# Experts 2 to 7: row tiles by way of DRAM and VectorE instead of TensorE's transposes

## The chip, the cores and the metric

The kernel runs on one core of a Trainium2 chip. The time is the device time of one execution in microseconds; a comparison goes by the median of several runs of each kernel on the same chip. Engines are named as in the profile: PE is TensorE (PEld its weight loads), DVE VectorE, ACT ScalarE, POOL GpSimd, and SP SyncE, which issues nearly all DMAs. Where the row of an engine ends in q (SPq, PEq), it is that engine's queue.

## What is computed

Three stages follow each other: linear attention, a mixture of eight experts with two experts per token, and a feed-forward block whose two weight matrices are given in 64-bit floats.

```python
def _moe_ref(x, w_gate, w_noise, noise, w1, w2):
    logits = x @ w_gate
    noisy_logits = logits + np.log1p(np.exp(x @ w_noise)) * noise
    top2 = np.argpartition(-noisy_logits, 2, axis=1)[:, :2]
    ...
    for e in range(E):
        for k in range(2):
            mask = top2[:, k] == e
            h = np.maximum(x[mask] @ w1[e], 0.0)
            out[mask] += top2_w[mask, k, None] * (h @ w2[e])

def _moe2_ref(x, w_in, w_out, g_ln):
    h = x @ w_in
    solu = h * softmax(h)
    ...
    return (layernorm(solu) * g_ln) @ w_out

def reference(...):
    x = attention(q, k, v)           # 2304 tokens, 512 features
    x = _moe_ref(x, ...)             # 8 experts, 512 -> 1024 -> 512
    return _moe2_ref(x, ...)         # 512 -> 1024 -> 512
```

## The kernel before

**Products.** A number is split into a high part (32 bits, rounded for TensorE, written by ScalarE) and a low part (the rest, by a VectorE subtraction), and a product is three matmuls: high by high, high by low, low by high.

**Experts.** Attention's result lies in DRAM (`xd`). Each expert has 640 slots in five tiles of 128 tokens. `gather_x` lets GpSimd fetch the 128 rows of a tile by an indirect DMA into a buffer `xg` (tokens on partitions, 512 features along the row). `xt_tile` calls `transpose_split`: four TensorE transposes of 128 by 128 by way of a PSUM bank `t`, then ScalarE writes the high part `xh` and VectorE the low part `xl`, features on partitions. `mm1(e, m)`, m = 0 to 7, is the first product: eight blocks of 128 of the 1024 hidden features, each two halves of 320 tokens with 12 matmuls. Behind each block ScalarE takes the relu (`hh`), and VectorE the rest (`hl`); only the latter frees the block's PSUM bank `a`, of which there are two. `mm2(e, a)`, a = 0 to 4, is the second product: 24 matmuls for one tile of tokens, whose result `yo` is copied by VectorE (even a) or ScalarE (odd a) and stored to DRAM (`yd`).

**Order.** The schedule is written out by hand: engines run their instructions in the order of the code. Attention, routing and expert 0 stand in a table (`ORDER`); then a loop runs experts 1 to 7. In step m of the first product stand `mm1(e, m)`, for m below 4 the split of a quarter of w2 and `load_w1(e + 1, m)`, for m below 5 `gather_x(e + 1, m)`, and from m = 3 on one piece of the decode (`next(bg)`). In step a of the second product stand `xt_tile(e + 1, a)`, `mm2(e, a)`, a piece of the decode, and for a below 4 the split of a quarter of w1 for the next expert and the load of a quarter of its w2.

**Decode.** `decode_all` turns the 64-bit w_in and w_out into 32-bit floats while the experts run: 16 tiles, each loaded by SyncE into one of two buffers `f`, worked on by nine VectorE instructions in four pieces (tiles `dec`) and stored to DRAM. The first piece issues the loads of the first two tiles, the second begins to work on the first of them. It is in expert 1, at m = 3 and 4.

**Buffers.** A ring hands out named buffers in turn, and an instruction that writes one waits until its last reader is through. `raw` (weights as loaded) is a ring of four, `xg` one of five, and `dec` takes three of a ring of four.

**Tail.** Behind the experts, the 18 token tiles of the feed-forward block already turn most of their tiles in another way: the tile is written to DRAM (`d_write`), read back in four pieces of 32 partitions (`d_read`), and turned by VectorE in blocks of 32 by 32 (`d_back`). The weights in that stage are loaded in the row order that goes with it.

Of the kernel before, what the change touches and what calls it, by code (L numbers as in the profile page):

```python
# [8 lines left out]
F32 = mybir.dt.float32  # L9
# [3 lines left out]
U32 = mybir.dt.uint32  # L13
# [7 lines left out]
NT, DM, FF, E = 2304, 512, 1024, 8  # L21
# [3 lines left out]
KD, KF = DM // 128, FF // 128  # L25
NA = 5
# [27 lines left out]

NP = 2

ORDER = """
F:100011101100000000100000000000101111 lk:0 lq:0 lkl:0 lk:1 kr:0 kmt:0 qm:0 lvl:0 km:0:0 klt:0 kl:0 km:0:1 kb:0
lk:2 kr:1 qs:0 lv:0 rz:0 ks:0 kmt:1 ksl:0 qe:0 kr:2 km:1:0 T:0 kmt:2 rz:1 km:1:1 C:0 kb:1 lkl:1 rz:2 T:1 km:2:0
# [25 lines left out]
def attn_moe_kernel(ctx: ExitStack, tc: tile.TileContext, q, k, v, w_gate, w_noise, noise,  # L85
                    w1, w2, w_in, w_out, g_ln, out, order=None, stop=False):
    nc = tc.nc
    V, A, P, T, SP = nc.vector, nc.scalar, nc.gpsimd, nc.tensor, nc.sync
# [5 lines left out]
    dram = ctx.enter_context(tc.tile_pool(name="dram", bufs=1, space=DRAM))  # L94
    sb = ctx.enter_context(tc.tile_pool(name="sb", bufs=1))

    def slot(tag, shape, dt, name):
        return sb.tile(shape, dt, tag=tag, name=name)

    def ring(*tags):  # L100
        state = [-1]

        def take(shape, dt, name):
            state[0] = (state[0] + 1) % len(tags)
            return slot(tags[state[0]], shape, dt, name)
        return take

    new_raw = ring("R2", "R3", "R0", "R1")
    new_row = ring("S0", "S2", "S4", "S1", "S3")
    new_out = ring("S9", "S8", "S10")  # L110
    new_s2 = ring("S5", "S6", "S7", "S11")
    psA = ctx.enter_context(tc.tile_pool(name="psA", bufs=2, space=PSUM))
    psB = ctx.enter_context(tc.tile_pool(name="psB", bufs=2, space=PSUM))
# [4 lines left out]
    tab = dram.tile([OVT * 128, 2], I32, name="tab")  # L118
    win32 = dram.tile([DM, FF], F32, name="win32")
    wout32 = dram.tile([FF, DM], F32, name="wout32")  # L120
    dd = {t: dram.tile([128, FF], F32, name=f"dd{t}") for t in range(NP, NC - 2)}

    def bank_t():
        return psT.tile([128, 512], F32, tag="t", name="t")
# [19 lines left out]

    def load_w1(e, j):
        t = new_raw([128, KD, 256], F32, "raw")
        src = win32 if e == E else w1[e]
        SP.dma_start(out=t, in_=src[:, 256 * j:256 * j + 256].rearrange("(k p) f -> p k f", p=128))
        raw[1, e, j] = t

    def load_w2(e, j):
        t = new_raw([128, 2, 512], F32, "raw")
        if e < E:
            SP.dma_start(out=t, in_=w2[e][256 * j:256 * j + 256, :].rearrange("(k p) d -> p k d", p=128))
        else:
            for g in range(4):
                r = 256 * g + 64 * j
                SP.dma_start(out=t[32 * g:32 * g + 32], in_=wout32[r:r + 64, :].rearrange("(k c) d -> c k d", c=32))
        raw[2, e, j] = t
# [26 lines left out]
    def dec_src(i):  # L186
        if i < 8:
            r, c = divmod(i, 2)
            return w_in, win32, slice(128 * r, 128 * r + 128), 512 * c
        return w_out, wout32, slice(128 * (i - 8), 128 * (i - 8) + 128), 0  # L190
# [7 lines left out]
    def decode(i):  # L198
        _, dst, rs, c0 = dec_src(i)
        t = d64.pop(i).rearrange("p (c w) -> p c w", w=2)  # L200
        lw, hw = t[:, :, 0], t[:, :, 1]
        a, b, c = (new_s2([128, 512], U32, f"dec{j}") for j in range(3))
        V.tensor_scalar(b, hw, 3, 0x3FFFFFF8, op0=OP.logical_shift_left, op1=OP.bitwise_and)
        V.scalar_tensor_tensor(a, hw, 0xC0000000, b, op0=OP.bitwise_and, op1=OP.bitwise_or)
        V.scalar_tensor_tensor(a, lw, 29, a, op0=OP.logical_shift_right, op1=OP.bitwise_or)
        yield

        V.tensor_scalar(b, lw, 0x1FFFFFFF, 6, op0=OP.bitwise_and, op1=OP.logical_shift_right)
        V.tensor_scalar(c, a, 0xFF800000, None, op0=OP.bitwise_and)
        V.tensor_tensor(b, b, c, op=OP.bitwise_or)  # L210
        yield
        af, bf, cf = (x.bitcast(F32) for x in (a, b, c))
        V.tensor_sub(bf, bf, cf)
        V.scalar_tensor_tensor(af, bf, 2.0 ** -23, af, op0=OP.mult, op1=OP.add)
        yield

        V.tensor_scalar(c, hw, 20, 0x7FF, op0=OP.logical_shift_right, op1=OP.bitwise_and)
        V.scalar_tensor_tensor(af, c, 896.5, af, op0=OP.is_ge, op1=OP.mult)
        SP.dma_start(out=dst[rs, c0:c0 + 512], in_=af)
# [245 lines left out]
    eTs, xs = {}, {}  # L465
# [68 lines left out]
    Gt = {}  # L534
# [170 lines left out]
    def count_overflow():  # L705
        ps = bank_t()[:, 0:E]
        count(ps, [M16[:, i] for i in range(NC)] + [skip], True, True)
        V.tensor_copy(CT, ps)
        o = const.tile([128, E], F32, name="ovc")
        m = const.tile([128, E], I32, name="ovm")  # L710
        s = const.tile([128, 1], F32, name="ovs")
        V.tensor_scalar(o, CT, -float(CAP), 0.0, op0=OP.add, op1=OP.max)
        V.tensor_scalar(o, o, 127.0, None, op0=OP.add)
        V.tensor_copy(m, o)
        V.tensor_scalar(m, m, 127, None, op0=OP.bitwise_and)
        V.tensor_sub(o, o, m)
        V.reduce_sum(s, o, axis=AX)
        V.tensor_scalar(novi, s, 1.0 / 128.0, None, op0=OP.mult)


    xg = {}

    def gather_x(e, a):
        t = new_row([128, DM], F32, "xg")
        c = E * a + e
        first = e == 0 and a < TA
        P.indirect_dma_start(out=t, out_offset=None, in_=xd[0:NRA, :] if first else xd, in_offset=bass.IndirectOffsetOnAxis(  # L727
            ap=idxA[:, a:a + 1] if first else idx[:, c:c + 1], axis=0))
        xg[e, a] = t

    def transpose_split(t, hi, lo):
        ps = bank_t()
        for kk in range(KD):
            T.transpose(ps[:, 128 * kk:128 * kk + 128], t[:, 128 * kk:128 * kk + 128], ident)  # L734
        pv = ps.rearrange("p (k t) -> p k t", k=KD)
        A.copy(hi, pv)  # L736
        V.tensor_sub(lo, pv, hi)  # L737

    XT = {}

    def xt_tile(e, a):
        if a == 0:
            XT[e] = (slot("XH", [128, KD, CAP], F32R, "xh"), slot("XL", [128, KD, CAP], F32R, "xl"))
        hi, lo = XT[e]
        transpose_split(xg.pop((e, a)), hi[:, :, 128 * a:128 * a + 128], lo[:, :, 128 * a:128 * a + 128])

    hT = {}

    def mm1(e, m):
        hi, lo = XT[e]  # L750
        pa = bank_a()
        j, o = m // 2, 128 * (m % 2)
        for n in range(2):
            for kk in range(KD):
                wh, wl = W1h[j][:, kk, o:o + 128], W1l[j][:, kk, o:o + 128]
                xh, xl = hi[:, kk, HC * n:HC * n + HC], lo[:, kk, HC * n:HC * n + HC]
                for s, (a, b) in enumerate(((wh, xh), (wh, xl), (wl, xh))):
                    T.matmul(pa[:, n, 0:HC], lhsT=a, rhs=b, start=(kk == 0 and s == 0),  # L758
                             stop=(kk == KD - 1 and s == 2))
        h, l = h_tiles(m)  # L760
        h2, l2 = (x.rearrange("p (n c) -> p n c", n=2) for x in (h, l))
        A.activation(out=h2, in_=pa[:, :, 0:HC], func=AF.Relu)  # L762
        V.scalar_tensor_tensor(l2, pa[:, :, 0:HC], 0.0, h2, op0=OP.max, op1=OP.subtract)  # L763
# [340 lines left out]
    def stepwise(f):  # L1104

        def step(*a):
            if a[-1] == 0:
# [13 lines left out]
                  lv2=lambda j: load_w2(1, j), hx=lambda a: gather_x(1, a), xu=lambda a: xt_tile(1, a))  # L1121
    for op in (order or ORDER).split():
        f, *a = op.split(":")
# [5 lines left out]
    for e in range(1, E):  # L1129
        for m in range(KF):  # L1130
            mm1(e, m)
            if m < 4:
                split_w2(e, m)
                load_w1(e + 1, m)
            if e + 1 < E and m < NA:
                gather_x(e + 1, m)
            if m >= 3:
                next(bg, None)
            if e == 2 and m == 5:
                pair_gates()  # L1140
                count_overflow()
        if stop:
            return
        for a in range(NA):
            if e + 1 < E:
                xt_tile(e + 1, a)
            mm2(e, a)
            if e < E - 1:
                next(bg, None)
                if a < 4:  # L1150
                    split_w1(e + 1, a)
                    load_w2(e + 1, a)
                continue
            gather_y(a)
            if a < 2:
                for j in (2 * a, 2 * a + 1):
                    split_w1(E, j)
                    load_w2(E, j)
            elif a == 2:
                next(bg, None)  # L1160
                combine(0)
                split_w2(E, 0)
            elif a == 3:
                x2_trans(0)
                combine(1)
                split_w2(E, 1)
# [69 lines left out]
```

## Time and profile before

| | us |
|---|---|
| median of 3 runs | 807.34 |
| lowest and highest | 806.57 and 809.58 |
| the profiled execution | 807.68 |
| its span, first to last instruction | 806.0 |
| TensorE busy in it | 758.2 |
| VectorE, ScalarE, GpSimd busy | 501.2, 293.8, 144.6 |

The span is what the trace covers; the profiled execution's own time has what lies around it too. The mean granted clock of TensorE is 0.982 of full speed. Matmuls overlap each other, so a matmul's duration is not what it costs in the stream; that is the distance between starts.

### The profile page before, as it was taken

Reading aid. Unit: us, or ns where it says so; the run is one execution under the profiler, and the core shown is the slowest. Engines: PE = TensorE matmul, PEld = TensorE weight load, DVE = VectorE, ACT = ScalarE, POOL = GpSimd, SP = SyncE. Lnnn points to the kernel's source line nnn. Section 1 sums busy time; section 2 is a strip of 40 time slices with the busy share of each in tenths; the row PEclk is TensorE's granted clock in tenths of the full one; section 3 lists DMA queues with packets and bytes.
Section 4 is the critical chain, followed back from the end, with each engine's and each line's share of the span. In section 5 each row is a group of like instructions: output and inputs, shape, how many; then the busy total and the mean of one; then the engine's idle time right before and its main releaser. Section 6 shows DMA issues by size and latency. Waiting matters only on the chain. (4 is left out here: it accounts for less than half of the span.)

```text
span 806.0 us, 12480 instructions
## 1 busy us (share of the span) xinstructions
PE 758.2 (94%) x4934; PEld 684.0 (85%) x4934; DVE 501.2 (62%) x884; ACT 293.8 (36%) x486; POOL 144.6 (18%) x130
## 2 busy tenths in 40 slices
PE   2877869999999999999999999999999999999997
PEld 1777867989789889889899899899898899989985
DVE  6998773334656656556556646546457767767661
ACT  1656531323223323223223232232345354444451
POOL 3684564020110110110200100000342111100000
PEclk9998888999999999999999999999999999999999
DMA  9973444265363454454543552432844545553311
GB/s 274 278 236 119 145 157 139 75 205 157 119 195 107 139 173 144 157 166 136 169 132 121 182 180 94 157 108 76 231 124 146 169 145 158 157 157 131 114 44 39
DMA packets 81534, 119.98 MB, mean 149 GB/s; under 512 B 14912, under 2 KB 52800, under 8 KB 81472
## 3 DMA queue, kind: packets, MB, share of 16 engines
q1 hardware_dynamic: 75392, 99.22, 38.6%
q0 software_dynamic: 6080, 19.93, 9.1%
q8 instruction: 39, 0.64, 0.3%
q14 instruction: 23, 0.19, 0.1%
HBM read 87.67 MB, written 31.46 MB: 148 GB/s over the span
## 5 line engine op out<-in xcount | busy, mean ns | idle before, releaser
L758 PE MATMUL a<-xh,w1h 128*128 128x320 f32 x448 | 138.5, 309 | 1.2 <-DVE hl L763 1.2
L758 PE MATMUL a<-xl,w1h 128*128 128x320 f32 x448 | 138.4, 309 | 0.0
L758 PE MATMUL a<-xh,w1l 128*128 128x320 f32 x448 | 138.3, 309 | 0.0
L794 PE MATMUL b<-w2h,hh 128*128 128x512 f32 x320 | 128.7, 402 | 0.0
L794 PE MATMUL b<-w2h,hl 128*128 128x512 f32 x320 | 126.7, 396 | 0.0
L794 PE MATMUL b<-w2l,hh 128*128 128x512 f32 x320 | 126.3, 395 | 0.0
L762 ACT ACTIVATE hh<-a 128x640 fp32r<-128x640 f32 x56 | 39.6, 707 | 159.8 <-PE a L758 159.8
L727 POOL DMA_INDIRECT xg<-xd,idx x38 | 40.7, 1071 | 304.1 <-PE t L734 294.3
L763 DVE SCALAR_TENSOR_TENSOR hl<-a,hh 128x640 fp32r<-128x640 f32 x56 | 46.1, 824 | 65.0 <-ACT hh L762 64.9
L758 PEld LDWEIGHTS a<-xh,w1h 128*128 128x128 f32 x448 | 84.2, 188 | 1.8 <-DVE hl L763 1.4
L758 PEld LDWEIGHTS a<-xl,w1h 128*128 128x128 f32 x448 | 84.1, 188 | 0.4
L758 PEld LDWEIGHTS a<-xh,w1l 128*128 128x128 f32 x448 | 84.2, 188 | 0.0
L817 POOL DMA_INDIRECT yg<-yd,posi x36 | 35.0, 973 | 208.6 <-DVE w1l L164 100.1
L794 PEld LDWEIGHTS b<-w2h,hl 128*128 128x128 f32 x320 | 60.0, 187 | 13.9
L794 PEld LDWEIGHTS b<-w2l,hh 128*128 128x128 f32 x320 | 60.2, 188 | 13.0
L794 PEld LDWEIGHTS b<-w2h,hh 128*128 128x128 f32 x320 | 60.2, 188 | 12.6
L164 DVE TENSOR_TENSOR w1l<-raw,w1h 128x1024 fp32r<-128x1024 f32 x32 | 38.9, 1222 | 33.4 <-ACT w1h L163 33.4
L842 PE MATMUL a<-w1h,x2h 128*128 128x256 f32 x288 | 57.5, 281 | 1.2 <-ACT x2h L736 0.7
L842 PE MATMUL a<-w1h,x2l 128*128 128x256 f32 x288 | 57.0, 279 | 0.0
L842 PE MATMUL a<-w1l,x2h 128*128 128x256 f32 x288 | 56.8, 278 | 0.0
L796 DVE COPY yo<-b 128x512 f32<-128x512 f32 x24 | 16.6, 692 | 64.2 <-PE b L794 64.2
L925 PE MATMUL b<-w2x,dT 128*128 128x512 f32 x216 | 54.3, 400 | 0.0
(209 smaller groups left out, 1399.3 us busy)
## 6 DMA issues: line engine op xcount, KB each, us to landing
raw<-in_moe_w_dram SPq DMA_DIRECT2D x64, 512.0 KB, 3.7
yd<-yo SPq DMA_DIRECT2D x40, 256.0 KB, 2.0
dd<-ed SPq DMA_DIRECT2D x14, 512.0 KB, 2.6
dq<-dd SPq DMA_DIRECT2D x56, 128.0 KB, 3.8
k<-in_k_dram SPq DMA_DIRECT2D x4, 1024.0 KB, 8.0
q<-in_q_dram SPq DMA_DIRECT2D x4, 1024.0 KB, 8.0
v<-in_v_dram SPq DMA_DIRECT2D x4, 1024.0 KB, 10.6
xd<-xr SPq DMA_DIRECT2D x8, 512.0 KB, 2.6
```

The lines of the kernel that those rows point to most:

```text
L164: (pick_engine(20 + j, P, V) if e == 0 else V).tensor_sub(W1l[j], t, W1h[j])
L727: P.indirect_dma_start(out=t, out_offset=None, in_=xd[0:NRA, :] if first else xd, in_offset=bass.IndirectOffsetOnAxis(ap=idxA[:, a:a + 1] ...
L758: T.matmul(pa[:, n, 0:HC], lhsT=a, rhs=b, start=(kk == 0 and s == 0), stop=(kk == KD - 1 and s == 2))
L762: A.activation(out=h2, in_=pa[:, :, 0:HC], func=AF.Relu)
L763: V.scalar_tensor_tensor(l2, pa[:, :, 0:HC], 0.0, h2, op0=OP.max, op1=OP.subtract)
L794: T.matmul(pb, lhsT=x, rhs=y, start=(kk == 0 and s == 0), stop=(kk == KF - 1 and s == 2))
L796: (A.copy if a % 2 else V.tensor_copy)(t, pb)
L817: P.indirect_dma_start(out=r, out_offset=None, in_=yd[0:n, :], in_offset=bass.IndirectOffsetOnAxis(ap=posi[:, c, j:j + 1], axis=0))
L842: T.matmul(pa[:, n, 256 * c:256 * c + 256], lhsT=x[:, kk, :], rhs=w[2 * n + c][:, kk, :], start=(kk == 0 and s == 0 and c == 0), stop=(kk ...
L925: T.matmul(pb, lhsT=x[:, kk, :], rhs=w, start=(kk == 0 and s == 0), stop=(kk == KF - 1 and s == 2))
```

## The change

For experts 2 to 7 (`EQ = 2`) a tile of rows takes another way to `xh` and `xl`. It is gathered into one of three other buffers (`new_hop`), written to a DRAM tile of its own (`write_x`), and read back in four pieces (`read_x`): the piece g of 32 partitions gets features 128 g to 128 g + 127 of all 128 tokens, in runs of 128 floats. VectorE turns the tile in blocks of 32 by 32 into `xt`, so that features stand on partitions, and the split reads `xt` in SBUF where it read PSUM. On partition 32 g + c, place k, stands feature 128 g + 32 k + c; `load_w1` for these experts therefore loads w1 in the same order, by four DMAs of 32 partitions where there was one of 128. The write of tile m - 1 and the reads of tile m - 3 stand in step m of the first product, behind the load of w1 and ahead of the decode. `decode` takes its result tile from S5 and S6 in turn, and its scratch tiles are always S7 and S11.

```diff
+EQ = 2
...
+    new_hop = ring("RH0", "RH1", "RH2")
...
+    xs_d = {(e, a): dram.tile([128, DM], F32, name=f"xs{e}_{a}") for e in range(EQ, E) for a in range(NA)}
...
-        src = win32 if e == E else w1[e]
-        SP.dma_start(out=t, in_=src[:, 256 * j:256 * j + 256].rearrange("(k p) f -> p k f", p=128))
+        src = (win32 if e == E else w1[e])[:, 256 * j:256 * j + 256]
+        if e < EQ or e == E:
+            SP.dma_start(out=t, in_=src.rearrange("(k p) f -> p k f", p=128))
+        else:
+            for g in range(4):
+                SP.dma_start(out=t[32 * g:32 * g + 32], in_=src[128 * g:128 * g + 128].rearrange("(k c) f -> c k f", c=32))
...
-        a, b, c = (new_s2([128, 512], U32, f"dec{j}") for j in range(3))
+        a, b, c = (slot(tag, [128, 512], U32, f"dec{j}") for j, tag in enumerate((("S5", "S6")[i % 2], "S7", "S11")))
...
-        t = new_row([128, DM], F32, "xg")
+        t = (new_row if e < EQ else new_hop)([128, DM], F32, "xg")
...
+    def write_x(e, a):
+        SP.dma_start(out=xs_d[e, a], in_=xg[e, a])
+
+    def read_x(e, a):
+
+        t = xg[e, a] = new_row([128, DM], F32, "xg")
+        for g in range(4):
+            SP.dma_start(out=t[32 * g:32 * g + 32].rearrange("i (b f) -> i b f", b=4),
+                         in_=xs_d[e, a].rearrange("(b i) f -> i b f", i=32)[:, :, 128 * g:128 * g + 128])
...
-        transpose_split(xg.pop((e, a)), hi[:, :, 128 * a:128 * a + 128], lo[:, :, 128 * a:128 * a + 128])
+        hi, lo = (x[:, :, 128 * a:128 * a + 128] for x in XT[e])
+        t = xg.pop((e, a))
+        if e < EQ:
+            transpose_split(t, hi, lo)
+            return
+        x = slot(("S12", "Gt")[a % 2], [128, KD, 4, 32], F32, "xt")
+        V.transpose(x.rearrange("p k b i -> p b k i"), t.rearrange("p (b k c) -> p b k c", b=4, k=KD))
+        x = x.rearrange("p k b i -> p k (b i)")
+        A.copy(hi, x)
+        V.tensor_sub(lo, x, hi)
...
+            if EQ <= e + 1 < E:
+                if 1 <= m < NA + 1:
+                    write_x(e + 1, m - 1)
+                if 3 <= m:
+                    read_x(e + 1, m - 3)
```

Two places show what it moves. On SyncE's queue, in expert 1 from the last load of w1 for expert 2 (m = 3) to the first loads of the decode; names in brackets are the counters that an issue waits for, DMAHW0 to DMAHW7 those of SyncE's transfers in turn, DMASW those of GpSimd's. Before:

```order
L148 DMA raw<-in_moe_w_dram 128x4x256 [waits DMAHW1_49,DVE_49]
L148 DMA raw<-in_moe_w_dram 128x4x256 [waits DMAHW2_49,DVE_49]
L195 DMA f_1930<-in_moe_w_in_dram 128x1024 [waits DMAHW3_49]
L195 DMA f_1932<-in_moe_w_in_dram 128x1024 [waits DMAHW4_49]
L219 DMA win_78<-dec_1963 128x512 [waits DMAHW5_49,DVE_49]
```

In the changed kernel:

```order
L156 DMA raw<-in_moe_w_dram 32x4x256 [waits DMAHW5_49,DVE_49]
L156 DMA raw<-in_moe_w_dram 32x4x256 [waits DMAHW6_49]
L156 DMA raw<-in_moe_w_dram 32x4x256 [waits DMAHW7_49]
L156 DMA raw<-in_moe_w_dram 32x4x256 [waits DMAHW0_49]
L740 DMA xs_2_82<-xg 128x512 [waits DMAHW1_49,DMASW4_49]
L746 DMA xg<-xs_0_80 32x4x128 [waits DMASW5_49,DMAHW2_49,DMASW0_49,PE_49]
L746 DMA xg<-xs_0_80 32x4x128 [waits DMAHW3_49]
L746 DMA xg<-xs_0_80 32x4x128 [waits DMAHW4_49]
L746 DMA xg<-xs_0_80 32x4x128 [waits DMAHW5_49]
L203 DMA f_1980<-in_moe_w_in_dram 128x1024 [waits DMAHW6_49]
L203 DMA f_1982<-in_moe_w_in_dram 128x1024 [waits DMAHW7_49]
```

One issue of w1 has become four, and a write and four reads have come between it and the loads `f`; each issue waits for the counter that the eighth issue before it used.

On VectorE, in the second product of expert 2, from the split of the first quarter of w1 to the subtraction of the third tile. Before:

```order
L213 TENSOR_TENSOR dec_2543<-dec_2543,dec_2544 128x512
L214 SCALAR_TENSOR_TENSOR dec_2542<-dec_2543,dec_2542 128x512
L164 TENSOR_TENSOR w1l_98<-raw,w1h_94 128x1024
L737 TENSOR_TENSOR xl<-t,xh 128x4x128
L217 TENSOR_SCALAR dec_2544<-f_2228 128x512
L218 SCALAR_TENSOR_TENSOR dec_2542<-dec_2544,dec_2542 128x512
L164 TENSOR_TENSOR w1l_99<-raw,w1h_95 128x1024
L737 TENSOR_TENSOR xl<-t,xh 128x4x128
```

In the changed kernel:

```order
L221 TENSOR_TENSOR dec_2637<-dec_2637,dec_2638 128x512
L222 SCALAR_TENSOR_TENSOR dec_2636<-dec_2637,dec_2636 128x512
L172 TENSOR_TENSOR w1l_128<-raw,w1h_124 128x1024
L768 STREAM_TRANSPOSE xt<-xg 128x4x4x32
L771 TENSOR_TENSOR xl<-xt,xh 128x4x128
L225 TENSOR_SCALAR dec_2638<-f_2288 128x512
L226 SCALAR_TENSOR_TENSOR dec_2636<-dec_2638,dec_2636 128x512
L172 TENSOR_TENSOR w1l_129<-raw,w1h_125 128x1024
L768 STREAM_TRANSPOSE xt<-xg 128x4x4x32
L771 TENSOR_TENSOR xl<-xt,xh 128x4x128
```

Ahead of each subtraction `xl` stands the transpose of the same tile, with nothing between the two.

## Rows read from the trace of the kernel before

**Rows 1.** The page, part 1: busy time of each engine, share, instructions.
```profile
PE 758.2 (94%) x4934; PEld 684.0 (85%) x4934; DVE 501.2 (62%) x884; ACT 293.8 (36%) x486; POOL 144.6 (18%) x130
```

**Rows 2.** Waits of TensorE, 200 to 560 us: us in total, times, longest.
```profile
PE a L758 <- DVE hl L763: 1.2, 1, 1.2
```

**Rows 3.** Timeline of TensorE: start, duration, engine, line, operation, names, shapes, count.
```profile
400.06 0.40 PE L794 MATMUL b<-w2h,hl 128*128 128x512 f32 x1
400.29 0.60 PE L734 MATMUL t<-ident,xg 128*128 128x128 f32 x4
...
400.96 0.39 PE L794 MATMUL b<-w2l,hh 128*128 128x512 f32 x1
```

**Rows 4.** The same timeline, expert 7's second product without transposes, first and next.
```profile
557.01 0.40 PE L794 MATMUL b<-w2h,hh 128*128 128x512 f32 x1
...
579.36 0.60 PE L734 MATMUL t<-ident,yg 128*128 128x128 f32 x4
```

**Rows 5.** Groups by line and shape: count, busy us, mean ns, idle before, releasers.
```profile
L737 DVE TENSOR_TENSOR xl<-t,xh 128x512 fp32r<-128x512 f32 x40 | 27.1, 685 | 1.5 <-ACT xh L736 1.5
...
L734 PE MATMUL t<-ident,xg 128*128 128x128 f32 x160 | 23.3, 272 | 1.0 <-DVE xl L737 1.0
...
L898 DVE STREAM_TRANSPOSE dq<-dq 128x1024 f32<-128x1024 f32 x14 | 17.4, 1245 | 0.7 <-issue 0.4
```

**Rows 6.** Timeline of all engines at one hand-over between experts.
```profile
406.51 0.59 ACT L796 COPY yo<-b 128x512 f32<-128x512 f32 x1 [4.99 <-PE b L794]
...
406.99 1.05 ACT L163 CAST w1h<-raw 128x1024 fp32r<-128x1024 f32 x1
...
407.94 0.59 ACT L736 CAST xh<-t 128x512 fp32r<-128x512 f32 x1
...
408.08 1.23 DVE L164 TENSOR_TENSOR w1l<-raw,w1h 128x1024 fp32r<-128x1024 f32 x1 [1.97 <-ACT w1h L163]
...
412.33 0.31 PE L758 MATMUL a<-xh,w1h 128*128 128x320 f32 x1
```

**Rows 7.** Timeline of VectorE in expert 1, at the first piece of the decode.
```profile
195.81 0.82 DVE L763 SCALAR_TENSOR_TENSOR hl<-a,hh 128x640 fp32r<-128x640 f32 x1 [1.36 <-ACT hh L762]
200.59 0.43 DVE L203 TENSOR_SCALAR dec<-f 128x512 uint32<-128x512 uint32 x1 [3.95 <-DMA f<-in_moe_w_in_dram]
...
202.39 0.82 DVE L763 SCALAR_TENSOR_TENSOR hl<-a,hh 128x640 fp32r<-128x640 f32 x1
```

**Rows 8.** Timeline of SyncE's queue in expert 1; a row spans several issues.
```profile
183.92 10.93 SPq L148 DMA_DIRECT2D raw<-in_moe_w_dram  x4
194.90 0.97 SPq L195 DMA_DIRECT2D f<-in_moe_w_in_dram  x2
```

**Rows 9.** Timeline of TensorE in expert 1, at its one wait.
```profile
201.62 0.31 PE L758 MATMUL a<-xl,w1h 128*128 128x320 f32 x1
201.77 0.30 PE L758 MATMUL a<-xh,w1l 128*128 128x320 f32 x1
203.26 0.42 PE L758 MATMUL a<-xh,w1h 128*128 128x320 f32 x1 [1.19 <-DVE hl L763]
```

**Rows 10.** Timeline of SyncE's queue in the tail: four-piece reads, a write.
```profile
662.75 1.75 SPq L892 DMA_DIRECT2D dq<-dd  x4
671.27 0.34 SPq L887 DMA_DIRECT2D dd<-ed  x1
```

**Rows 11.** DMA issues by line: count, KB each, median us to landing.
```profile
dq<-dd SPq DMA_DIRECT2D x56, 128.0 KB, 3.8
```

**Rows 12.** Windows: stretch, length, busy (instructions) of each engine, clock, DMA share, GB/s.
```profile
100.00:105.00 5.00, 1.62 (x23) 1.46 (x20) 4.93 (x11) 1.82 (x6) 2.18 (x1) 0.89 0.94 335
105.00:110.00 5.00, 5.00 (x25) 5.00 (x25) 1.57 (x5) 1.32 (x2) 2.71 (x2) 0.50 0.47 185
110.00:115.00 5.00, 4.82 (x38) 4.61 (x37) 4.20 (x5) 2.18 (x5) 5.00 (x3) 0.93 0.31 105
177.00:207.00 30.00, 28.81 (x196) 28.45 (x194) 14.96 (x19) 9.28 (x12) 0.00 (x0) 1.00 0.45 143
```

More of the change, by code (lines that the diff above doesn't have):

```diff
@@ L743, in xt_tile @@
             XT[e] = (slot("XH", [128, KD, CAP], F32R, "xh"), slot("XL", [128, KD, CAP], F32R, "xl"))
-        hi, lo = XT[e]
-        transpose_split(xg.pop((e, a)), hi[:, :, 128 * a:128 * a + 128], lo[:, :, 128 * a:128 * a + 128])
+        hi, lo = (x[:, :, 128 * a:128 * a + 128] for x in XT[e])
[8 more added lines that the diff above has]
+        V.tensor_sub(lo, x, hi)
     hT = {}
```

## The prediction

> **What bounds the kernel now.** I read the page first: TensorE is busy for 758.2 of the 806.0 us, VectorE for 62% [rows 1]. The table of waits says what that share is made of in the experts' part: from 200 to 560 us TensorE waited once, for 1.2 us, on VectorE [rows 2]. So from the second expert on the time is the sum of TensorE's own instructions, and an edit gains what it takes out of that stream and loses what it makes TensorE wait for. I therefore read three places: the stream of TensorE around a group of transposes [rows 3, 4], the engines that must be done when one expert's first product follows the second product of the expert before [rows 6], and the one wait that is already there [rows 7 to 9].
>
> **What is removed.** Experts 2 to 7 have five token tiles each, so 30 groups of four transposes (120 of the 160 of that form [rows 5]) leave TensorE. Their own duration, 272 ns, overlaps their neighbours, so I price a group by the starts around it: the matmul ahead starts at 400.06, the transposes at 400.29, and the second matmul behind them at 400.96 [rows 3]. Without transposes 96 matmuls of this kind take from 557.01 to 579.36, 0.2328 us each [rows 4]. The 0.90 us from 400.06 to 400.96 would have been two such steps, 0.466; a group costs 0.434 us. Thirty make **13.0 us**, all on the path.
>
> The Trainium skill (TensorE: Matmul & The Clock Gate, Part 4: PE-mode transpose) gives about 275 ns for one transpose inside a kernel. By that figure 120 of them would be an estimated 33.0 us; this case's trace agrees on the duration of one, 272 ns, but not on the price in the stream, and the stream decides.
>
> **What VectorE and ScalarE get.** VectorE's 32 by 32 transpose of 1024 columns takes 1245 ns [rows 5]; half the columns I take at 0.62 us. The split into high and low part stays (0.59 us on ScalarE [rows 6], 0.685 on VectorE [rows 5]), but it now starts from VectorE's result, and VectorE stands while ScalarE rounds, since nothing lies between the two in its order. That is some 1.3 us more for VectorE per tile, 6.5 us in an expert of about 56 us (eight blocks of 24 matmuls of 0.15 [rows 9], five of 24 of 0.2328), where it has idle time. What counts is the hand-over: the last tile (a = 4) is converted during the last product with w2. There the low part of w1 runs from 408.08 to 409.31, held up by ScalarE, which first copies a result (406.51) and then rounds w1 (406.99) [rows 6]. Behind it come the transpose 0.62, the rounding 0.59, the subtraction 0.68 and some 0.1 for hand-shakes: done at 411.3. TensorE reaches the next expert at 412.33 [rows 6] less 0.43 for that step's own group, 411.9, and it needs the last tile only for the second half of the first output block, 12 matmuls of 0.15 us later, at 413.7. The spare is 2.4 us, so I put this at **nothing**. Were that cover gone, each us would count six times, once for each of experts 2 to 7.
>
> **What the DMAs get.** A row tile is now gathered into one of three buffers, written to DRAM and read back in four pieces. The reads and writes of the tail are the nearest rows: 1.75 us of SyncE's queue for four reads, 0.34 for a write [rows 10], 3.8 us from issue to landing of a read [rows 11]. The reads are issued in steps 3 to 7 of the first product, the first of them is wanted behind step 7 and then one per 5.6 us. Five steps of 3.5 us make over 17 us, so the round trip is hidden, as are the gathers, which no longer wait for TensorE. The loads of w1, now in four pieces, are wanted eight steps later, 28 us. The new decode buffers take waits for the decode's own stores from VectorE, and these hide under TensorE already: nothing.
>
> **What SyncE's queue costs, once.** The first load for the decode stands behind all of this. In expert 1 the fourth w1 issue ends at 194.85 and the two f loads follow from 194.90 [rows 8]. VectorE, in order, meets the first decode instruction right behind the relu split of 195.81, stands until that load has landed (the instruction starts at 200.59), and only then gets to the next relu split at 202.39 [rows 7], which frees the PSUM bank that TensorE waits for: TensorE's next matmul starts 1.49 us behind that of 201.77 instead of 0.15 [rows 9]. So this load is on the path already, with no spare, and what delays it TensorE stands for. Ahead of it come three more w1 issues, one write and four reads, 7 x 0.44 + 0.34 = 3.4 us; and in the order every issue of this queue waits for the transfer eight issues before it. For the f load that is the second w1 piece, issued near 194.9 and landing 3.8 later, at 198.7. I take **3.9 us** of delay, with the load's own time unchanged (200.55 less 194.90, 5.65). The bounds are 2.5 (the w1 load that it shares the DMA engines with is mostly gone by then) and 5.0 (the reads and writes behind it share them instead).
>
> TensorE then stands for 1.2 plus 3.9, about 5 us. What such a pause does to its clock can be read earlier: from 100 to 105 us TensorE was busy for 1.62, and the granted clock was 0.89 there, 0.50 in the next 5 us and 0.93 in the 5 behind [rows 12]. In time at the lower of the two levels (1.2 against 2.4 GHz) that is 1.1 + 5.0 + 0.7 = 6.8 us, with the engine at work again. The 1.2 us pause left the clock at 1.00 from 177 to 207 us [rows 12]. A pause of 5 us is on the side of the first, so I add 6.8 us at half speed, **3.4 us**; the bounds are 0 and 3.4.
>
> **Sum.** 13.0 removed, 3.9 and 3.4 added: 5.7 us less. The profiled execution is 807.68 (span 806.0) and would be 802.0; from the median of 807.34 it is **801.6 us**.
>
> **The rivals.** First, the pause comes and the clock holds: nothing in the experts' part shows a pause this long, and the matmuls around it are dense. 807.34 - 13.0 + 3.9 = 798.2.
> Second, the f load isn't later for VectorE (the queue is faster than the tail's rows, or the load lands sooner): 794.3. Against it stand the eight issues, each with a price in the rows.
> Third, the one on the slow side: the hand-over fails. Place: the start of the first product of experts 2 to 7. Mechanism: the last tile's chain of transpose, rounding and subtraction ends later than the spare of 2.4 us allows, because a read lands late or VectorE falls behind with the decode. An overrun of x costs 6x on top of the 801.6; it decides from x = 1.0, where the gain is gone, and at 2 us it is 813.6.
> Fourth, each transpose counts with its whole duration, with the same losses: 807.34 - 120 x 0.272 + 7.3 = 782.0. [Rows 3, 4] speak against it.
> The Trainium skill (VectorE: DVE Perf Modes, Rules for kernel authors) says to use TensorE for a 128 by 128 transpose where PSUM will do as its destination. That is a rule against this change, and it comes out right here if the third rival does; no run so far shows which.
>
> **How the numbers follow.** Chances: the forecast 0.54 (799.5 to 803.7 by the bounds of its delay and a little of its clock), the clock holds 0.20, no longer pause 0.11, the hand-over lost 0.08, smaller delays at several hand-overs that eat most of the gain 0.06, the whole duration 0.01. The range takes the first three with their bounds: 794 to 804.5. A measurement of this kernel tells some 0.5% from no change, 4 us, so faster means under 803.3: most of the forecast (0.46 of 0.54), with 0.20, 0.11 and 0.01, makes 0.78. Same: 0.08 of the forecast and the 0.06, 0.14. Slower: 0.08.
>
> **What would show it.** Right: no transposes of gathered rows on TensorE behind expert 1's own, 0.2328 us per step right across the tiles of the second products, no wait of TensorE at the six hand-overs, VectorE's transposes of 512 columns near 0.62 us. For the loss: one wait of TensorE on VectorE's relu split in expert 1 of about 5 us, ahead of it VectorE standing 7 to 8 us for the f load, which is issued near 198.8, and a granted clock under 1.00 just behind. Wrong: waits of TensorE on xh or xl (the hand-over), or a VectorE transpose that stands for a DMA; or a wait in expert 1 that is no longer than before, and a time near 794.

## The result, and the profile after

The changed kernel takes 799.0 us (median of 6 runs), the kernel before 807.7 beside it: the ratio is 0.990, with a 95% interval from 0.988 to 0.9921, which is 6.4 to 9.7 us less. That is faster by the bound of 4 us and inside the range; the forecast of 801.6 was 2.6 us too high. One of the six runs took 851.3 us, at a mean granted clock of 0.844 where the others have 0.975 to 0.983, and the ratio leaves it out. The profiled execution took 799.15 us, with a span of 797.4 where 806.0 was.

The page, part 1, of the kernel after (it answers to [rows 1]):

```profile
PE 744.6 (93%) x4814; PEld 671.7 (84%) x4814; DVE 522.8 (66%) x914; ACT 296.1 (37%) x486; POOL 143.0 (18%) x130
```

TensorE has 120 instructions fewer, VectorE 30 more. Of the groups by line and shape, these are what is left of the transposes, and what came:

```profile
L752 PE MATMUL t<-ident,xg 128*128 128x128 f32 x40 | 5.4, 274 | 1.0 <-DVE xl L755 1.0
...
L768 DVE STREAM_TRANSPOSE xt<-xg 128x512 f32<-128x512 f32 x30 | 21.1, 704 | 0.0
L771 DVE TENSOR_TENSOR xl<-xt,xh 128x512 fp32r<-128x512 f32 x30 | 20.8, 693 | 21.0 <-ACT xh L770 21.0
```

The 40 are those of experts 0 and 1. TensorE's waits from 200 to 560 us, as in [rows 2]:

```profile
PE a L784 <- DVE hl L789: 5.9, 1, 5.9
```

So there is no wait at any of the six hand-overs, and one in expert 1, longer than before. The starts of four products cut the span into stretches (timeline of TensorE; first products at L784, second at L820):

```profile
176.47 0.31 PE L784 MATMUL a<-xh,w1h 128*128 128x320 f32 x1
...
212.38 0.39 PE L820 MATMUL b<-w2h,hh 128*128 128x512 f32 x1
...
381.21 0.40 PE L820 MATMUL b<-w2h,hh 128*128 128x512 f32 x1
...
409.14 0.31 PE L784 MATMUL a<-xh,w1h 128*128 128x320 f32 x1
...
549.49 0.40 PE L820 MATMUL b<-w2h,hh 128*128 128x512 f32 x1
```

The second product between 381.21 and 409.14 has 120 matmuls, 0.2328 us each, right across its five tiles. The last row is the place of [rows 4], 557.01. In the trace of before the first two places lie at 177.27 and 206.89.

| stretch | before | after | moved |
|---|---|---|---|
| ahead of expert 1 | 177.27 | 176.47 | -0.80 |
| first product of expert 1 | 29.62 | 35.91 | +6.29 |
| from there to expert 7's second product | 350.12 | 337.11 | -13.01 |
| the rest, to the span's end | 248.99 | 247.91 | -1.08 |
| span | 806.0 | 797.4 | -8.6 |

The first and the last stretch hold nothing that the change touches. In the traces of the kernels below, most of which share the code of both, expert 1 starts between 175.1 and 179.1 us, and the last stretch takes between 247.5 and 248.3. So 1.9 of the 8.6 us is what two executions differ by, and the change itself made -6.7.

Now the place of the loss, as in [rows 7, 8]. SyncE's queue and VectorE in expert 1 of the kernel after (SPq rows are issues, one row for several in a row):

```profile
193.68 1.85 SPq L156 DMA_DIRECT2D raw<-in_moe_w_dram  x4
195.63 0.38 SPq L740 DMA_DIRECT2D xs<-xg  x1
196.19 2.47 SPq L746 DMA_DIRECT2D xg<-xs  x4
198.70 1.02 SPq L203 DMA_DIRECT2D f<-in_moe_w_in_dram  x2
199.82 0.47 SPq L740 DMA_DIRECT2D xs<-xg  x1
200.47 3.07 SPq L746 DMA_DIRECT2D xg<-xs  x4
```

```profile
195.01 0.82 DVE L789 SCALAR_TENSOR_TENSOR hl<-a,hh 128x640 fp32r<-128x640 f32 x1 [1.36 <-ACT hh L788]
204.54 0.43 DVE L211 TENSOR_SCALAR dec<-f 128x512 uint32<-128x512 uint32 x1 [8.71 <-DMA f<-in_moe_w_in_dram]
...
206.34 0.82 DVE L789 SCALAR_TENSOR_TENSOR hl<-a,hh 128x640 fp32r<-128x640 f32 x1
```

Against the relu split ahead of it (195.81 in [rows 7], 195.01 here) the f load is issued 4.60 us later than before: 1.5 of that by w1's four pieces, 3.1 by the write and the reads. It takes 5.84 us from issue to use, where it took 5.69. TensorE, at the same place, and the clock in windows around it (columns as in [rows 12]):

```profile
200.97 0.30 PE L784 MATMUL a<-xh,w1l 128*128 128x320 f32 x1
207.21 0.64 PE L784 MATMUL a<-xh,w1h 128*128 128x320 f32 x1 [5.94 <-DVE hl L789]
207.64 0.47 PE L784 MATMUL a<-xl,w1h 128*128 128x320 f32 x1
207.91 0.47 PE L784 MATMUL a<-xh,w1l 128*128 128x320 f32 x1
```

```profile
200.00:205.00 5.00, 1.27 (x9) 1.01 (x7) 0.43 (x1) 0.70 (x1) 0.95 (x1) 0.88 0.98 272
205.00:210.00 5.00, 2.79 (x10) 2.79 (x11) 4.89 (x9) 0.00 (x0) 0.99 (x1) 0.50 0.68 220
210.00:215.00 5.00, 5.00 (x27) 4.51 (x27) 2.26 (x4) 0.70 (x1) 1.18 (x1) 0.93 0.77 209
```

Time at the lower level is 1.2 + 5.0 + 0.7, near 6.9 us. But the fall began in the pause, and only from 207.21 to 210.58 did it meet work: 12 steps in 3.37 us (0.267 each behind the first) that take 0.147 each at the upper level. It cost 3.37 - 12 x 0.147 = 1.6 us, the wait the other 4.7 of the 6.29.

### The profile page after: what moved, and what is told of

It is laid out like the page before. It is cut to its first block, busy times and chain, and to the rows that moved or that the text cites. A ratio compares the mean times of both kernels' runs of the same rounds, so it can differ in the third digit from the quotient of the medians.

```text
span 797.4 us, 12599 instructions
## 1 busy us (share of the span) xinstructions
PE 744.6 (93%) x4814; PEld 671.7 (84%) x4814; DVE 522.8 (66%) x914; ACT 296.1 (37%) x486; POOL 143.0 (18%) x130
## 5 line engine op out<-in xcount | busy, mean ns | idle before, releaser
L784 PE MATMUL a<-xh,w1h 128*128 128x320 f32 x448 | 139.4, 311 | 5.9 <-DVE hl L789 5.9
L784 PE MATMUL a<-xl,w1h 128*128 128x320 f32 x448 | 139.1, 311 | 0.0
L784 PE MATMUL a<-xh,w1l 128*128 128x320 f32 x448 | 139.1, 310 | 0.0
L820 PE MATMUL b<-w2h,hl 128*128 128x512 f32 x320 | 126.8, 396 | 0.0
L820 PE MATMUL b<-w2l,hh 128*128 128x512 f32 x320 | 126.4, 395 | 0.0
L820 PE MATMUL b<-w2h,hh 128*128 128x512 f32 x320 | 126.3, 395 | 0.0
L735 POOL DMA_INDIRECT xg<-xd,idx x38 | 38.0, 999 | 327.2 <-DMA xs<-xg 315.6
L784 PEld LDWEIGHTS a<-xh,w1h 128*128 128x128 f32 x448 | 84.9, 189 | 6.5 <-DVE hl L789 6.2
L784 PEld LDWEIGHTS a<-xl,w1h 128*128 128x128 f32 x448 | 84.8, 189 | 0.4
L784 PEld LDWEIGHTS a<-xh,w1l 128*128 128x128 f32 x448 | 84.8, 189 | 0.0
L820 PEld LDWEIGHTS b<-w2l,hh 128*128 128x128 f32 x320 | 60.1, 188 | 14.2
L820 PEld LDWEIGHTS b<-w2h,hh 128*128 128x128 f32 x320 | 60.2, 188 | 13.8
L820 PEld LDWEIGHTS b<-w2h,hl 128*128 128x128 f32 x320 | 60.0, 187 | 13.9
L770 ACT CAST xh<-xt 128x512 fp32r<-128x512 f32 x30 | 18.6, 621 | 94.5 <-DVE xt L768 94.5
L951 PE MATMUL b<-w2h,dT 128*128 128x512 f32 x144 | 48.1, 395 | 0.0
```

The source lines that it names most:

```text
L770: A.copy(hi, x)
L820: T.matmul(pb, lhsT=x, rhs=y, start=(kk == 0 and s == 0), stop=(kk == KF - 1 and s == 2))
L951: T.matmul(pb, lhsT=x[:, kk, :], rhs=w, start=(kk == 0 and s == 0), stop=(kk == KF - 1 and s == 2))
```

## The experiments

Every kernel is compared with the kernel before on the same chip (807.5 to 808.5 us there). The theory: one load, the first f, lies on the path in expert 1 and is pushed back by issues ahead of it, so that its place in the queue decides. The rivals: the sharing of the DMA engines delays it, or w1's pieces of 32 partitions do; and for the gain, that hand-overs or buffers matter more than they show. Three expectations use letters: A is the sharing, B the place in the queue, C the pieces.

### The f load ahead of the loop

The first piece of `decode_all` (two loads, nothing else) is run before expert 1; once on the changed kernel, once on the kernel before.

```diff
     bg = decode_all()
+    next(bg)
```

> The changed kernel with the first piece of the decode (the two f loads, no other work) issued ahead of the loop over the experts instead of in step 3 of expert 1. Theory: all that the change loses is the f load behind w1 pieces, write and reads on SyncE's queue; expert 1's first product then takes 28.2 us instead of 35.9 (no wait of TensorE, no lower clock), and the kernel 799.0 - 7.7 = 791.3 us. Rival: the delay comes from the DMA traffic as a whole or from VectorE's added work, so that the pause turns up at another place; then expert 1 or a hand-over shows a wait of TensorE of some us and the time stays over 796.

> The kernel before with the same single edit: first piece of the decode ahead of the loop. Theory: its pause on the f load was 1.45 us in all (29.6 against 28.2 us for expert 1's first product), so 807.7 - 1.45 = 806.3 us. Rival (the load's place matters little): 807.7.

The changed kernel came to 791.5 us, ratio 0.980 [0.978, 0.981], the kernel before to 805.3, 0.996 [0.994, 0.997]. SyncE's queue and the two ends of expert 1's first product on TensorE, changed kernel with this edit:

```profile
179.68 0.93 SPq L203 DMA_DIRECT2D f<-in_moe_w_in_dram  x2
```

```profile
176.07 0.31 PE L784 MATMUL a<-xh,w1h 128*128 128x320 f32 x1
...
204.23 0.40 PE L820 MATMUL b<-w2h,hh 128*128 128x512 f32 x1
```

28.16 us, the same in both kernels: no wait, no clock fall. All that expert 1 lost goes with the time of this one load. The kernel before gains 3.2 us where 1.45 was expected; its product gives back 1.46 (29.62 to 28.16), and in the traces the rest lies where the edit changes nothing. Between these two kernels stand 13.85 us, the price of the 30 groups (13.0) within what executions differ by. This is the best kernel of the study, 17 us ahead of the kernel before.

### Is it the place in the queue?

The write and the four reads of step 3 stand ahead of the f loads. First they are put behind them:

```diff
+            if e == 1 and m == 3:
+                next(bg)
...
-            if m >= 3:
+            if m >= 3 and (e, m) != (1, 3):
                 next(bg, None)
```

> The changed kernel with only the order within step 3 of expert 1 changed: the two f loads stand ahead of the write and the four reads, but still behind the four pieces of w1. Theory: of the 3.8 us by which the issue was late, three pieces at 0.44, 1.3 us, remain; TensorE waits 1.2 + 1.3 = 2.5 us instead of 5.9, and the kernel takes 799.0 - 3.4 - (0 to 1.6 for the clock) = 794.0 to 795.6. Rival (the DMA engines are what holds the load up, since write and reads run beside it in any order): the load takes longer than 5.7 us from its issue, and over 797.

797.9 us, 0.986 [0.985, 0.988]; the expectation failed, and what its rival named came. The product takes 35.88 us, as in the changed kernel:

```profile
193.63 1.77 SPq L156 DMA_DIRECT2D raw<-in_moe_w_dram  x4
195.44 1.19 SPq L203 DMA_DIRECT2D f<-in_moe_w_in_dram  x2
196.73 1.12 SPq L740 DMA_DIRECT2D xs<-xg  x1
198.04 2.60 SPq L746 DMA_DIRECT2D xg<-xs  x4
```

```profile
204.23 0.43 DVE L211 TENSOR_SCALAR dec<-f 128x512 uint32<-128x512 uint32 x1 [8.44 <-DMA f<-in_moe_w_in_dram]
```

The loads leave 3.3 us earlier, but now it takes 8.8 us until VectorE goes on, not 5.8: at 204.23, where it was 204.54. What follows the loads in the queue isn't the whole reason, since a write and four reads stand right behind them in the changed kernel too (199.82 and 200.47 there). What differs besides is that w1's pieces were issued only 1.8 us ahead, not 5.0. Two kernels take that apart. In the first, the second f load moves one piece later:

```diff
-        load_f64(1)
         yield
         for i in range(16):
-            yield from decode(i)
+            for n, _ in enumerate(decode(i)):
+                if i == 0 and n == 0:
+                    load_f64(1)
+                yield
```

> As f_ahead, but only the first of the two f loads stands there; the second is issued one piece of the decode later. Theory A (sharing): the first load no longer shares the engines with the second, of 128 rows of 4 KB too, and lands about 2 us sooner; pause 5.7 - 2.3 = 3.4 us, 797.9 - 2.3 = 795.6, down to 794 if the clock falls for less. Theory B (place in the queue) and C (w1 pieces): no change against f_ahead, 797.9.

798.8 us, 0.990 [0.986, 0.993], not the 795.6 of A: the four runs, from 796.5 to 801.6, show no gain over f ahead. The trace does: issue at 196.35, use at 203.29, 6.9 us; the product takes 33.77, 2.1 less. Without the second f load beside it, the first comes 1.85 us sooner. In the second kernel, all writes and reads for expert 2 stand behind the f loads, in steps 4 to 7 and 5 to 7, and the gathers that need a written tile's buffer move with them:

```diff
-            if EQ <= e + 1 < E:
+            if e == 1:
+                for i in {4: (0, 1), 5: (2,), 6: (3,), 7: (4,)}.get(m, ()):
+                    write_x(2, i)
+                for i in {5: (0,), 6: (1,), 7: (2, 3, 4)}.get(m, ()):
+                    read_x(2, i)
+            elif e + 1 < E:
```

> The changed kernel with the writes and reads of expert 2's tiles moved back within expert 1 (writes in steps 4 to 7, reads in steps 5 to 7), so that the two f loads follow the four w1 pieces directly and no write, read or fourth and fifth gather shares the DMA engines with them. Theory A (sharing: with the f loads issued early in f_ahead they still took 8.8 us, because write, gathers and reads ran beside them): the load takes 5.7 us from its issue again, TensorE's pause is 1.2 + 1.3 = 2.5 us and expert 1's first product 31 us instead of 35.9: 799.0 - 4.9 = 794.1, or 795.7 with some lower clock. Theory B (only the place in SyncE's queue counts): as f_ahead, which had the same place, 797.9. Theory C (the w1 pieces of 32 partitions hold the load up): as f_ahead too, with 8 us or more from issue to landing.

795.5 us, 0.985 [0.982, 0.988], as A, the sharing, has it (794.1 to 795.7). VectorE there:

```profile
202.18 0.43 DVE L211 TENSOR_SCALAR dec<-f 128x512 uint32<-128x512 uint32 x1 [4.95 <-DMA f<-in_moe_w_in_dram]
```

Both f ahead and this kernel issue the loads 19.0 us into the product, but here use comes 5.3 us behind the issue, and the product takes 32.14. The second f load is there, and three writes leave 1.9 us behind the first (from 198.76); the reads and the gathers are away. This move gives back 3.5 us, the second load's 1.85, more than the 3 us together, so the two can't be added up. What is common to the five kernels shows in the windows from the issue of the first f load to its use (last columns: clock, DMA share, GB/s; rows of before, after, f ahead, one load ahead, and writes later, in this order):

```profile
194.90:200.59 5.69, 5.69 (x40) 5.69 (x40) 0.82 (x1) 1.41 (x2) 0.00 (x0) 1.00 0.82 268
```

```profile
198.70:204.54 5.84, 2.57 (x18) 2.31 (x16) 0.00 (x0) 0.70 (x1) 0.95 (x1) 0.94 0.94 268
```

```profile
195.44:204.23 8.79, 5.78 (x40) 5.52 (x38) 0.35 (x2) 1.41 (x2) 0.94 (x1) 0.99 0.93 274
```

```profile
196.35:203.29 6.94, 5.81 (x40) 5.54 (x38) 0.37 (x1) 1.41 (x2) 0.94 (x1) 1.00 0.97 252
```

```profile
196.86:202.18 5.32, 5.32 (x38) 5.32 (x37) 0.38 (x1) 0.71 (x1) 0.00 (x0) 1.00 0.97 262
```

The DMA engines move 252 to 274 GB/s in each of them, and the load's time goes by how much is moved: 1.52, 1.57, 2.41, 1.75 and 1.39 MB. In f ahead, by the sizes of the packets in the trace, 1.36 of the 2.41 MB belong to w1, a gather, writes and reads. So the place in the queue and the sharing both hold, one in the place of the other. With the writes and reads ahead, the load leaves late, when w1 is through; put ahead of them, it meets w1 besides and lands late; only when reads and gathers are away does most of the time come back.

### One expert fewer, and w1 in pieces

With `EQ = 3` expert 2 goes the old way, so expert 1 issues neither writes nor reads. Then the same with expert 2's w1 in four pieces of 32 partitions (in the old order of rows):

```diff
-EQ = 2
+EQ = 3
```

> The changed kernel with EQ = 3: expert 2's tiles are turned by TensorE as before, experts 3 to 7 by VectorE; nothing is written or read back during expert 1. Theory (the loss is one pause in expert 1, the gain 0.434 us for each of 25 groups): 807.7 - 10.85 = 796.9 us, faster than the changed kernel by 2.1 though it converts fewer experts, with expert 1's first product at 29.6 us. Rival (gain and loss both belong to each expert converted): five sixths of the 8.7 us, 800.5.

```diff
-        if e < EQ or e == E:
+        if e == 2:
+            for g in range(4):
+                SP.dma_start(out=t[32 * g:32 * g + 32], in_=src.rearrange("(k p) f -> p k f", p=128)[32 * g:32 * g + 32])
+        elif e < EQ or e == E:
```

> As eq3 (nothing written or read back in expert 1), but w1 of expert 2 is loaded by four DMAs of 32 partitions in the old row order. Theory A (sharing, and w1's bytes are the same): the f load starts to move when w1 is through, as in eq3, and lands at most 0.5 us later; expert 1's first product 29.7 to 30.2 us against 29.7, the kernel 797.3 to 797.8. Theory B (place in the queue): issued 1.3 us later, lands 1.3 us later, 31.0 us and 798.6. Theory C (pieces of 32 partitions are slow): over 32 us, over 800.

797.3 us, 0.986 [0.984, 0.987], and 797.4, 0.988 [0.985, 0.990]. The first is no slower than the changed kernel, with 25 groups taken out instead of 30: expert 1's product takes 29.69 us, and TensorE's wait is 1.3. The pieces make the wait 1.9 and the product 31.85, more than A and B had. Of these 2.2 us some 0.6 is the wait: the load leaves 1.4 us later (195.55, 19.0 us into the product), but takes 5.0 us, not 5.8. The rest is the clock, which fell for 3.4 us behind the 1.9 us pause. So of the change's 4.7 us longer wait, the pieces of w1 are some 0.6; C is no explanation. The new order of w1's rows was not tried by itself.

### How much spare has the hand-over?

VectorE turns each expert's last tile three or seven times instead of once.

```diff
-        V.transpose(x.rearrange("p k b i -> p b k i"), t.rearrange("p (b k c) -> p b k c", b=4, k=KD))
+        for _ in range(7 if a == NA - 1 else 1):
+            V.transpose(x.rearrange("p k b i -> p b k i"), t.rearrange("p (b k c) -> p b k c", b=4, k=KD))
```

> As turn7 with three transposes of the last tile instead of seven: 2 x 0.75 = 1.5 us more per hand-over. Theory (spare 2.35 us; in turn7 4.48 us more made each first product 2.14 us longer, so 2.34 were spare): nothing, 799.0 us, first products of experts 3 to 7 at 28.16 us. Rival (every us of VectorE counts): 6 x 1.5 = 9 us more, 808.

> The changed kernel with VectorE's transpose of the last tile (a = 4) of experts 2 to 7 done seven times instead of once (the same result each time). In the profile of the changed kernel the last subtraction ends 2.35 us ahead of where TensorE needs it. Six more transposes at 0.62 to 0.70 us are 3.7 to 4.2 us: theory (the spare is 2.35 us and only the rest counts, once per expert): 6 x 1.4 to 6 x 1.85 = 8 to 11 us more, 807 to 810, with a wait of TensorE on xl of 1.4 to 1.9 us at each of six hand-overs. Rival (VectorE's lateness is caught by the buffers, TensorE never waits there): 799.

Three: 801.0 us, 0.991 [0.988, 0.994]. TensorE waits at no hand-over, and the first products of experts 3 to 7 keep 28.16 us to 0.01; expert 2's, which holds other work besides, takes 28.74, as in the changed kernel. The 2 us above the changed kernel lie ahead of expert 1 and in it (it starts at 177.77, and its product takes 36.77), not at the hand-overs. Seven: 816.0 us, 1.010 [1.007, 1.013], slower than before. VectorE at one hand-over, and TensorE's waits from 215 to 560 us:

```profile
418.09 5.18 DVE L769 STREAM_TRANSPOSE xt<-xg 128x512 f32<-128x512 f32 x7
```

```profile
PE a L785 <- ACT xh L771: 7.8, 6, 1.3
PE a L785 <- DVE xl L772: 1.9, 6, 0.3
```

Seven transposes take 5.18 us, 4.48 more than one. The first products of experts 3 to 7 take 30.30 us, 2.14 more than 28.16: the difference, 2.34, is the spare. Behind the wait in expert 2 alone the clock fell, for some 3.4 us, and there it is 3.68. The expected 807 to 810 failed: the added transposes were priced too short (3.7 to 4.2 us, not 4.48) and the clock was left out, together some 3 us; another 3.7 us in the profiled execution lie ahead of expert 2's first product, where the edit changes nothing. The mechanism is the one of the slow rival, flat up to the spare, then six times.

### The decode's buffers

The two halves of the change are parted: the new buffers alone (`EQ = 8`: no expert is converted), and everything but them.

```diff
-EQ = 2
+EQ = 8
```

> The decode's new tiles alone: EQ = 8, no expert takes the new way. Theory: as the kernel before, 807.9 us, with VectorE's waits on its own decode stores gone and TensorE's stream the same. Rival (they were worth something): under 806.

```diff
-        a, b, c = (slot(tag, [128, 512], U32, f"dec{j}") for j, tag in enumerate((("S5", "S6")[i % 2], "S7", "S11")))
+        a, b, c = (new_s2([128, 512], U32, f"dec{j}") for j in range(3))
```

> The changed kernel with the decode's tiles from the ring of four as before. Theory (the waits of VectorE on the decode's own stores come back, some 7 us in all as in the kernel before, and hide under TensorE): 799.0 us, no new wait of TensorE. Rival (these stores now stand behind reads and writes in SyncE's queue, VectorE falls behind and loses the hand-overs): 801 or more, with waits of TensorE on xl.

Alone they give 807.0 us, 0.999 [0.997, 1.000]: nothing, as predicted. Without them the change takes 820.1 us, 1.017 [1.011, 1.022], 21 us more than with them, where 799.0 was expected. VectorE's and TensorE's waits from 200 to 560 us, without them:

```profile
DVE dec L211 <- DMA win<-dec: 11.6, 2, 6.6
DVE dec L211 <- DMA wout<-dec: 10.4, 2, 7.2
...
DVE dec L211 <- DMA f<-in_moe_w_in_dram: 8.8, 1, 8.8
DVE dec L211 <- DMA xg<-xs: 8.7, 1, 8.7
```

```profile
PE a L784 <- DVE hl L789: 14.6, 3, 6.1
PE b L820 <- DVE hl L789: 5.7, 2, 4.1
```

The last of VectorE's rows is one such case in full. VectorE, SyncE's queue, and the DMA issues from 383 to 396 us (count, KB, us from issue to landing):

```profile
383.56 0.69 DVE L226 SCALAR_TENSOR_TENSOR dec<-dec,dec 128x512 f32<-128x512 uint32 x1
...
395.40 0.43 DVE L211 TENSOR_SCALAR dec<-f 128x512 uint32<-128x512 uint32 x1 [8.69 <-DMA xg<-xs]
```

```profile
386.45 1.92 SPq L746 DMA_DIRECT2D xg<-xs  x4
388.47 0.49 SPq L227 DMA_DIRECT2D win<-dec  x1
```

```profile
win<-dec SPq DMA_DIRECT2D x1, 256.0 KB, 6.8
```

A piece ends at 384.25; its store leaves only at 388.47, behind the reads, and lands 6.8 us later, at 395.3. The next piece, which in a ring of four takes that result's buffer, starts at 395.40 (the row names reads as its releaser; what frees the buffer is the store). Behind it on VectorE stands the relu split that TensorE waits for. Four products lengthen: expert 2's second from 27.9 to 29.7, expert 3's first from 28.2 to 35.1, expert 4's second from 27.9 to 34.8, expert 5's first from 28.2 to 35.5, and in the last three the clock falls.

### Expert 1 converted as well

With the f loads early, `EQ = 1` takes five more groups from TensorE.

```diff
-EQ = 2
+EQ = 1
...
-... gx:4 xt:2 xt:3 xt:4 m2:1 mb:0 mb:1 hx:0 mb:2 hx:1 mb:3 lv1:2
+... gx:4 hx:0 hx:1 hx:2 xt:2 xt:3 xt:4 m2:1 mb:0 wx:0 mb:1 wx:1 hx:3
...
+    next(bg)
```

> f_early with expert 1 converted too (EQ = 1; its gathers, writes and reads stand in the table of expert 0, w1 of expert 1 in four pieces). Theory: five more groups of four transposes leave TensorE at 0.434 us, 791.5 - 2.2 = 789.3 us, if the round trips hide under expert 0's products as they do later. Rival: the round trips or VectorE's work are on the path while expert 0 runs, where TensorE waits for engines already: TensorE waits on xh or xl ahead of expert 1 for more than 2.2 us and the time is over 791.5.

797.7 us, 0.986 [0.983, 0.989], 6 us behind the f loads early alone. TensorE's and VectorE's waits, 165 to 560 and 165 to 300 us:

```profile
PE a L784 <- ACT xh L770: 4.7, 1, 4.7
```

```profile
DVE xt L768 <- DMA xg<-xs: 6.2, 2, 4.6
```

The expected 789.3 failed, and its rival came: in expert 0 the round trip is not hidden: the transposes wait for the reads, TensorE for them, and expert 1's first product takes 35.92 us, with 6.8 us at the lower clock.

## Why the prediction was right, step by step

**Removed, 13.0 us: right.** The stretch that holds all 30 groups is 13.01 us shorter. The Trainium skill (VectorE: DVE Perf Modes, Rules for kernel authors) would keep a 128 by 128 transpose on TensorE where its result may go to PSUM; here the measurement decides the other way. VectorE's turn takes 0.704 us, longer than the 0.434 that a group cost TensorE, and yet the change gains, because TensorE bounds this stretch and VectorE is busy for 66% of the span.

**The hand-over costs nothing: right.** The turn takes 0.70 us where 0.62 was taken. At one hand-over the last tile's subtraction starts at 407.86 and takes 0.69 us, and TensorE wants the tile at 410.90 (timeline of all engines, after):

```profile
407.86 0.69 DVE L771 TENSOR_TENSOR xl<-xt,xh 128x512 fp32r<-128x512 f32 x1 [0.69 <-ACT xh L770]
...
410.90 0.31 PE L784 MATMUL a<-xh,w1h 128*128 128x320 f32 x1
```

That is 2.35 us of spare against the 2.4 of the forecast, and seven turns measured 2.34. The slow rival was rightly named, with its place and its sixfold price. It would have taken more than three further turns to fill the spare (2.35 / 0.70).

**The wait in expert 1: right in place and kind, mis-sized.** Forecast: 3.9 us longer; measured 4.7, within the bounds of 2.5 and 5.0. VectorE stood for 8.71 us, not 7 to 8. The 4.60 us of later issue is the term that was short: the four reads took 2.47 us of the queue, not the 1.75 of the tail's row. The f load's own time was unchanged (5.84 against 5.69), but that is partly luck: the step named two opposite bounds, and both came. By the packets between issue and use, w1's 0.52 MB of the kernel before are gone, and 0.60 MB of reads, write and gather have taken their place. Sharing was thus more than a bound: in f ahead it alone makes the same wait once the queue does not.

**The clock, 3.4 us: the fall right, its price half.** It fell for 6.8 to 6.9 us, as read from [rows 12]. The step that failed is "with the engine at work again": half of the fall lay in the pause and cost nothing. 1.6 us was paid. How much of a fall lies in the pause isn't fixed: with three turns, 6.8 us at the lower level behind a pause of 6.1 cost some 2.5 (36.77 - 28.16 - 6.1).

**The sum.** -13.0 + 3.9 + 3.4 = -5.7 forecast, -13.0 + 4.7 + 1.6 = -6.7 measured. The medians differ by -8.7; in the two profiled executions, each within 0.2 us of its median, the 2 us between are the stretches that the change does not touch. So the closeness of the time owes something to luck: 0.8 us too little for the wait and 1.8 too much for the clock partly cancel. The median lies just under 799.5, the lower end that the forecast's own bounds gave (the upper, 803.7, does not follow from them: 5.0 of delay makes 802.7). "The clock holds" (798.2) is nearer to the median, but the clock did not hold.

**The round trip hidden: right for experts 1 to 6,** where no transpose waits for a read. With expert 1 converted, expert 0 would have to hide it, and does not.

**The buffers, "nothing": right alone, wrong as a reason.** "These hide under TensorE already" was read from the traffic of the kernel before. With 27 writes and 116 reads from 200 to 560 us on the same queue a store leaves later (4.2 us behind its piece, and 6.8 us to land, in the case shown), and the old ring would cost 21 us, more than the whole gain. The time of the forecast did not depend on it, because the change brings the buffers along; but a reader who took the sentence at its word and left them out would have had a slower kernel.

What stays open: how the 8.8 us of f ahead divide between w1's pieces, the second f load, the gather, the writes and the reads. No run takes away one of the last three alone.

## What to carry to other kernels

Price an instruction taken from a dense stream by the starts around it, not by its duration, and look for what takes over the work only where the next stage begins. When DMAs are added to an in-order queue, look first for the load that is already waited for with no spare, and move that one load far ahead: here one line was worth some 7.5 us, nearly as much as the change without it. A few places ahead were worth little, because the load shares the DMA engines with all that is in flight. A buffer that is reused behind a store is priced under the new traffic, not the old.

## What the runs showed of the hardware

The first f load took 5.3 to 5.8 us from issue to use in the kernel before, the changed one and the one with later writes, and 8.8 us in f ahead. The DMA engines moved 262 to 274 GB/s meanwhile in each, and 1.39 to 1.57 MB in the first three against 2.41 in f ahead.

The clock held at 1.00 behind pauses of 1.2 and 1.3 us in the same dense stream, and fell for 3.4 us behind pauses of 1.9, 2.2 and 3.8. That is one pause of each length, not a rule: six pauses of 1.3 and 0.3 us, with one matmul between, at the hand-overs with seven turns were followed by one fall.
